# Weights handed out in 42 single pieces, and a first half batch whose operands are written in place, in a three-stage fp32 kernel

## The chip, the core and the metric

The kernel runs on one core of one Trainium2 chip. The metric is the device time of one execution in microseconds (us). Five engines work side by side, each through its own instructions in order: PE (matrix products; its weight loads are shown as PEld), DVE (vector), ACT (scalar), POOL (GpSimd) and SP, which here only issues the DMA transfers.

## The reference, cut to what matters

Inputs are float32 or, for the weights, float64 in effect (pairs of 32-bit words). Batch 4, sequence 576, 8 heads of 64, so 512 channels.

```
attn  = softmax(mask(q k^T / 8)) v                 # windowed, half the heads dilated
x     = attn as [4, 576, 512];  xp = x one row later in the sequence
xk    = mu_k x + (1 - mu_k) xp ;  xr = mu_r x + (1 - mu_r) xp
k     = relu(xk @ w_k)           # 512 -> 1024
y     = sigmoid(xr @ w_r) * ((k * k) @ w_v)        # 512 -> 512, 1024 -> 512
u     = y + (y^T U V)^T
out   = u + relu(u @ w_ch1) @ w_ch2                # 512 -> 2048 -> 512
```

## The kernel before, in words

**Stages.** The second part (r, k, v products) works on eight half batches c = 0 to 7 of 288 rows. A half batch has 20 quanta of PE work in a list (`quanta`, L525): four for r, eight for k, eight for v. Beside them run the attention of the 32 units (`attend`, L405; a unit is one pair of heads and one part of one batch) and the unpacking of the weights (`cv_bits`, L291: one ACT and four DVE instructions, L305 to L312, for a piece of 128x512). After half batch 7 comes the third part (`ch1`, `ch2`, from L688), whose weights were unpacked earlier to DRAM (`w2f`) and are read back and divided by `load_w2`.

**Two precisions.** A product of half batch 0 is one fp32 product (`mm1`, L280). It shows in the trace as two matmul instructions. From half batch 1 on each operand is divided into a high part (an ACT copy, L266) and a low part (a subtraction, L261 on POOL or L263 on DVE), and a product is three fast ones (`mm3`, L272 to L274, and L590 to L592 for v). So the 20 weight pieces of part two (4 for r, 8 for k, 8 for v) stay whole until half batch 0 has used them, and are divided for half batch 1 (`split_weight`, L331): the list `SPLIT` says after which quantum, counted from the start of half batch 1, and `SPLIT_ENG` on which engine the subtraction runs (POOL for all).

**Storage.** All operands of the products lie in one tile, `arena`, at fixed columns. In half batch 0 an unpacked piece is carried there by a transfer (L327), a mix of x by another (L520), a square of k by another (L570). The unpacked piece waits in one of three buffers `w32`, the mix in one of two `m`, the square in one of two `k2`, until its transfer has landed.

**The order around the change.** Operations are first listed in program order, each with an estimated price, and then `plan` (L129) puts them in an order per engine: it looks at most `WINDOW` operations past the oldest one not yet placed, and takes a later operation only where it can start `SLACK` ns sooner. The engines then follow that order. In the list, six steps (L790 to L795) come ahead of the quanta: each starts an attention unit, unpacks up to one more piece, and from the third step on mixes x for one pair of heads, for r and for k. Then L797 to L813 go through the quanta of half batches 0 to 6; in half batch 0 `CONV0` says how many pieces must be unpacked ahead of each quantum (7, 8, ... 20), and a new unit starts at every fifth quantum. An r quantum needs all four mixes for r and one column block of all four r weights:

```
acc = rk(XR0, [WR0 + (p // 2) * SLOT + (p % 2) * CW + o * P for p in range(NPAIR)])      # L553
dma(P * CW * 4, lambda: nc.sync.dma_start(lo, x()), kx, cols_of(col + 2 * CW, CW))      # L327
dma(P * HS * 4, lambda: nc.sync.dma_start(hi, m()), [(m,)], cols_of(c_hi, HS))          # L520
dma(P * HS * 4, lambda: nc.sync.dma_start(hi, k2()), [(k2,)], cols_of(c_hi, HS))        # L570
```

Other lines that the prediction names: L419 (scores of a unit), L464 and L475 (its transposes and its product with v), L429 (its row minimum on DVE), L454 (its normalization on POOL), L514 (a mix), L554 (an r product copied out of PSUM), L563 and L564 (relu and square of a k product), L288 and L402 (loads of packed weights and of q, k).

Of the kernel before, what the change touches and what calls it, by code (L numbers as in the profile page):

```python
# [16 lines left out]
P = 128  # L17
# [25 lines left out]
SLOT = 2048  # L43
WR0 = 0
XR0 = WR0 + 2 * SLOT
WK0 = XR0 + 8 * HS
XK0 = WK0 + 4 * SLOT
WV0 = XK0 + 8 * HS
K20 = WV0 + 4 * SLOT
ARENA = 15 * SLOT  # L50
assert K20 + 16 * HS <= ARENA

# [8 lines left out]
WHOLE = 1  # L61
# [13 lines left out]
def tile_attention_mix_channel(  # L75
# [10 lines left out]
    arena = cp.tile([P, ARENA], F32R, name="arena")  # L86
# [38 lines left out]

    def cols_of(c0, n):
        return [("arena", k) for k in range(c0 // 32, (c0 + n) // 32)]

    def plan():  # L129
# [43 lines left out]
        def ready(o):  # L173
            t = 0.0
            for d in o.deps:
                if d.done is None:
                    return None
                t = max(t, d.done + 40)
            for x in o.tiles:
                if x.ops[0] is not o and x.ops[0].done is None:  # L180
                    return None
            for x in o.first:
                if x.at and x.line[x.at - 1].ops[0].done is None and x.line[x.at - 1].ops[0] is not o:
                    return None
                ends = sorted((x_end(y) for y in x.line[max(0, x.at - 16) : x.at]), reverse=True)
# [105 lines left out]
    def cv_bits(raw, n):  # L291
        xt_ = Lazy([P, CW], F32, "w32", "w32", 3)
# [24 lines left out]
    def hi_lo(n, x, kx, c_hi, c_lo, eng):  # L317

        hi, lo = arena[:, c_hi : c_hi + n], arena[:, c_lo : c_lo + n]
        copy(n, lambda: hi, x, kx, cols_of(c_hi, n))  # L320
        sub(eng, n, lambda: lo, x, lambda: f32(hi), kx + cols_of(c_hi, n), cols_of(c_lo, n))

    def cv_weight(raw, col, whole):
        x, kx = cv_bits(raw, CW)
        if whole:
            lo = f32(arena[:, col + 2 * CW : col + 3 * CW])
            dma(P * CW * 4, lambda: nc.sync.dma_start(lo, x()), kx, cols_of(col + 2 * CW, CW))  # L327
        else:
            hi_lo(CW, x, kx, col, col + 2 * CW, "POOL")

    def split_weight(col, eng):  # L331

        lo = f32(arena[:, col + 2 * CW : col + 3 * CW])
        hi_lo(CW, lambda: lo, cols_of(col + 2 * CW, CW), col, col + 2 * CW, eng)
# [23 lines left out]
    first_slot = [Lazy([P, CW], F32R, "pr", f"w2_{j}", 4) for j in range(4)]  # L358

    def w2_part(i, part):  # L360

        if i == 0:
            return first_slot[part]()
        c = (i - 1) * SLOT + part * CW
        return arena[:, c : c + CW]

    def w2_keys(i, *parts):
        if i == 0:
            return [(first_slot[part],) for part in parts]
        return [k for part in parts for k in cols_of((i - 1) * SLOT + part * CW, CW)]  # L370

    def load_w2(i, eng):
        st = Lazy([P, 2 * CW], F32, "w64", "wst", 4)
        dma(P * CW * 8, lambda: nc.sync.dma_start(st(), w2f[i]), [("w2f", i, 0), ("w2f", i, 1)], [(st,)])
        if i == 0:
            for j in range(2):
                x = lambda j=j: st()[:, j * CW : (j + 1) * CW]
                copy(CW, lambda j=j: first_slot[j](), x, [(st,)], [(first_slot[j],)])
                sub(eng, CW, lambda j=j: first_slot[2 + j](), x, lambda j=j: f32(first_slot[j]()),
                    [(st,), (first_slot[j],)], [(first_slot[2 + j],)])  # L380
        else:
            c = (i - 1) * SLOT
            hi_lo(2 * CW, lambda: st(), [(st,)], c, c + 2 * CW, eng)
# [21 lines left out]
    def attend(u):  # L405
# [18 lines left out]
        pe(nw * 82, qk, [(raw, "qk")], [(sc,)], "qk")  # L424
# [56 lines left out]
        pe(nw * 58, pv, [(pts, 0), (raw, "v")] + ([(pts, 1)] if nw == 5 else []), [(ov,)], "pv")  # L481
# [19 lines left out]
    def mix(c, p, which):  # L501
# [6 lines left out]
        base = XK0 if which == "k" else XR0  # L508
        if (c, p) not in dd:
# [15 lines left out]
    def quanta(c):  # L525
        b, half = divmod(c, 2)
        whole = c < WHOLE
        mm = mm1 if whole else mm3
# [3 lines left out]
        vacc = {}  # L532

        def x_parts(base, p):
            return arena[:, base + p * HS : base + (p + 1) * HS], arena[:, base + (4 + p) * HS : base + (5 + p) * HS]

        def w_keys(w):
            return (cols_of(w, P) if not whole else []) + cols_of(w + 2 * CW, P)

        def x_keys(base, p, lo=4):  # L540
            return cols_of(base + p * HS, HS) + (cols_of(base + (lo + p) * HS, HS) if not whole else [])

        def rk(base, ws):
            acc = bank("M")
            trips = [
                (arena[:, w : w + P], arena[:, w + 2 * CW : w + 2 * CW + P], *x_parts(base, p)) for p, w in enumerate(ws)
            ]
            keys = [k for p, w in enumerate(ws) for k in w_keys(w) + x_keys(base, p)]
            pe(quantum_ns, lambda: mm(acc()[:, :HS], trips), keys, [(acc,)], mode)
            return acc  # L550
# [9 lines left out]
        def k_tile(o):  # L560
            acc = rk(XK0, [WK0 + p * SLOT + o * P for p in range(NPAIR)])
            rt, k2 = Lazy([P, HS], F32, "rt", "rt", 2), Lazy([P, HS], F32, "k2", "k2", 2)
            act(HS, lambda: nc.scalar.activation(rt(), acc()[:, :HS], AF.Relu), [(acc,)], [(rt,)], psum=True)  # L563
            dve(HS, lambda: nc.vector.scalar_tensor_tensor(  # L564
                out=k2(), in0=acc()[:, :HS], scalar=0.0, in1=rt(), op0=ALU.max, op1=ALU.mult),
                [(acc,), (rt,)], [(k2,)], two=True, psum=True)
            c_hi, c_lo = K20 + o * HS, K20 + (8 + o) * HS
            if whole:
                hi = f32(arena[:, c_hi : c_hi + HS])
                dma(P * HS * 4, lambda: nc.sync.dma_start(hi, k2()), [(k2,)], cols_of(c_hi, HS))  # L570
            else:
                hi_lo(HS, lambda: k2(), [(k2,)], c_hi, c_lo, "DVE" if o in K2DVE else "POOL")

        def v_part(o, part):
# [4 lines left out]
            ws = [WV0 + (j // 2) * SLOT + (j % 2) * CW + o * P for j in js]  # L579

            def run():
                a = acc()[:, :HS]
                for j, w in zip(js, ws):
                    wh, wl = arena[:, w : w + P], arena[:, w + 2 * CW : w + 2 * CW + P]
                    xh = arena[:, K20 + j * HS : K20 + (j + 1) * HS]
                    xl = arena[:, K20 + (8 + j) * HS : K20 + (9 + j) * HS]
                    if whole:
                        nc.tensor.matmul(a, lhsT=f32(wl), rhs=f32(xh), start=(j == 0), stop=(j == 7))  # L588
                        continue
                    nc.tensor.matmul(a, lhsT=wh, rhs=xh, start=(j == 0), stop=False)  # L590
                    nc.tensor.matmul(a, lhsT=wl, rhs=xh, start=False, stop=False)  # L591
                    nc.tensor.matmul(a, lhsT=wh, rhs=xl, start=False, stop=(j == 7))  # L592

            keys = [k for j, w in zip(js, ws) for k in w_keys(w) + x_keys(K20, j, 8)]
            pe(quantum_ns, run, keys, [(acc,)], mode)
# [9 lines left out]
        q = [lambda o=o: r_tile(o) for o in range(4)]  # L605
# [136 lines left out]
    cols = [WR0 + j * SLOT for j in range(2)] + [WK0 + j * SLOT for j in range(4)] + [WV0 + j * SLOT for j in range(4)]  # L742
# [5 lines left out]
    for i, j in places:  # L748
        jobs.append((w1raw[i][:, j * CW : (j + 1) * CW], CW, lambda raw, c=cols[i] + j * CW: cv_weight(raw, c, WHOLE > 0)))
# [39 lines left out]

    for t in range(FIRST + 2):  # L790
        next_unit()
        convert_to(t + 1)
        if 0 <= t - 2 < NPAIR:
            mix(0, t - 2, "r")
            mix(0, t - 2, "k")  # L795
    divided = 0
    for c in range(NCH - 1):  # L797
        cur = quanta(c)
        for n in range(NQ):
# [4 lines left out]
            cur[n]()  # L804
# [134 lines left out]
```

## Time and profile before

| | us |
|---|---|
| median of 3 runs | 825.28 (825.14 to 825.81) |
| the profiled execution's own time | 826.75 |
| its span, first to last instruction | 825.0 |
| PE busy | 788.4 (96%) |
| DVE / ACT / POOL busy | 386.6 / 326.0 / 220.6 |

The profile is one execution. The page gives busy time by engine and, in 40 slices of 20.6 us, the busy share in tenths. Other views list the instructions in order of time with the idle time ahead of each and what ended it, group them by line and shape, total the waits by engine and line, and cut the span into stretches. PE's matmuls are pipelined, so a busy PE is not PE at its peak.

### The profile page before, as it was taken

To read this page: it belongs to the slowest core of one execution; us is meant where nothing else is said; L and a number is where in the kernel's file an instruction comes from. 1 tells how busy PE (TensorE), PEld (TensorE's weight loads), DVE (VectorE), ACT (ScalarE), POOL (GpSimd) and SP (SyncE) were. 2 spreads that over 40 slices of the span, in tenths; PEclk is the share of its full clock that TensorE was granted. 3 is DMA by queue.
4 is the path that set the end of the run, shared out by engine and by line. 5 is a ranking of instruction groups with operands and counts; after the bars stand their busy time and mean duration, and the time that the engine had idled before them with its cause. 6 is when DMAs were issued, how large, how long until landed. Compare 5 with 4: busy or idle time off the path is not lost.

```text
span 825.0 us, 16083 instructions
## 1 busy us (share of the span) xinstructions
PE 788.4 (96%) x6360; PEld 752.9 (91%) x6360; DVE 386.6 (47%) x996; ACT 326.0 (40%) x848; POOL 220.6 (27%) x240
## 2 busy tenths in 40 slices
PE   4749899999999999999999999999999999999998
PEld 4527599899999999999999999999999999999998
DVE  4978778888797875345512222222222122221211
ACT  4525777575757575746411221212212112121111
POOL 1202996354545353558110010100001000110000
PEclk9999999999999999999999999999999999999999
DMA  9997434747575645043700002000020000000000
GB/s 274 278 320 251 140 122 152 236 156 222 176 227 163 223 140 182 1 131 131 237 1 29 2 1 87 1 2 29 2 73 15 1 30 1 11 19 2 29 1 29
DMA packets 39900, 85.14 MB, mean 103 GB/s; under 512 B 4496, under 2 KB 14864, under 8 KB 39824
## 3 DMA queue, kind: packets, MB, share of 16 engines
q1 hardware_dynamic: 39824, 84.10, 31.3%
q8 instruction: 50, 0.82, 0.4%
q14 instruction: 26, 0.21, 0.1%
HBM read 58.66 MB, written 17.83 MB: 93 GB/s over the span
## 4 chain that ended last, share of the span: by engine, by line
PE 92%; DMA 3%; DVE 2%; ACT 1%; issue 1%; POOL 0%; SPq 0%; ACTq 0%; POOLq 0%
PE psM L272 14%; PE psM L274 14%; PE psM L273 14%; PE psS L720 8%; PE psS L722 8%; PE psS L721 8%; PE psM L590 4%; PE psM L591 3%; PE psM L592 3%; PE psS L419 3%; PE psM L280 3%; PE psS L475 2%; PE psS L464 2%; PE psM L588 2%; DMA raw<-qk 1%; PE psM L631 1%
## 5 line engine op out<-in xcount | busy, mean ns | idle before, releaser
L700 ACT ACTIVATE ch<-psM 128x288 fp32r<-128x288 f32 x128 | 52.8, 412 | 325.4 <-PE psM L274 325.3
L701 DVE SCALAR_TENSOR_TENSOR cl<-psM,ch 128x288 fp32r<-128x288 f32 x128 | 58.4, 456 | 248.1 <-ACT ch L700 248.1
L720 PE MATMUL psS<-ch,arena 128*128 128x288 f32 x480 | 143.8, 299 | 0.0
L272 PE MATMUL psM<-uh,arena 128*128 128x288 f32 x480 | 142.3, 297 | 0.0
L722 PE MATMUL psS<-cl,arena 128*128 128x288 f32 x480 | 142.0, 296 | 0.0
L721 PE MATMUL psS<-ch,arena 128*128 128x288 f32 x480 | 141.7, 295 | 0.0
L274 PE MATMUL psM<-ul,arena 128*128 128x288 f32 x480 | 141.5, 295 | 0.0
L273 PE MATMUL psM<-uh,arena 128*128 128x288 f32 x480 | 141.4, 295 | 0.0
L261 POOL TENSOR_TENSOR ul<-u,uh 128x288 fp32r<-128x288 f32 x32 | 25.8, 807 | 322.3 <-ACT uh L266 322.3
L272 PE MATMUL psM<-arena 128*128 128x288 f32 x336 | 102.9, 306 | 0.2 <-ACT arena L266 0.2
L274 PE MATMUL psM<-arena 128*128 128x288 f32 x336 | 99.6, 296 | 0.3 <-POOL arena L261 0.3
L273 PE MATMUL psM<-arena 128*128 128x288 f32 x336 | 99.8, 297 | 0.0
L720 PEld LDWEIGHTS psS<-ch,arena 128*128 128x128 f32 x480 | 90.3, 188 | 1.1 <-issue 1.1
L273 PEld LDWEIGHTS psM<-uh,arena 128*128 128x128 f32 x480 | 90.7, 189 | 0.0
L274 PEld LDWEIGHTS psM<-ul,arena 128*128 128x128 f32 x480 | 90.5, 189 | 0.0
L721 PEld LDWEIGHTS psS<-ch,arena 128*128 128x128 f32 x480 | 90.4, 188 | 0.0
L272 PEld LDWEIGHTS psM<-uh,arena 128*128 128x128 f32 x480 | 90.2, 188 | 0.0
L722 PEld LDWEIGHTS psS<-cl,arena 128*128 128x128 f32 x480 | 90.2, 188 | 0.0
L590 PE MATMUL psM<-arena 128*128 128x288 f32 x224 | 68.9, 307 | 0.0
L261 POOL TENSOR_TENSOR arena<-m,arena 128x288 fp32r<-128x288 f32 x56 | 50.0, 903 | 64.1 <-ACT arena L266 57.3
L591 PE MATMUL psM<-arena 128*128 128x288 f32 x224 | 66.0, 295 | 0.0
L592 PE MATMUL psM<-arena 128*128 128x288 f32 x224 | 65.8, 294 | 0.0
(100 smaller groups left out, 1529.4 us busy)
## 6 DMA issues: line engine op xcount, KB each, us to landing
w<-w2raw SPq DMA_DIRECT2D x32, 512.0 KB, 5.4
w<-w1raw SPq DMA_DIRECT2D x20, 512.0 KB, 6.1
w2f<-w SPq DMA_DIRECT2D x32, 256.0 KB, 3.4
wst<-w2f SPq DMA_DIRECT2D x16, 512.0 KB, 4.0
raw<-qk SPq DMA_DIRECT2D x16, 320.0 KB, 3.6
arena<-w SPq DMA_DIRECT2D x20, 256.0 KB, 4.8
ytmp<-y SPq DMA_DIRECT2D x32, 144.0 KB, 2.8
yb<-ytmp SPq DMA_DIRECT2D x4, 1152.0 KB, 6.4
```

What stands on the lines that cost most here:

```text
L261: op("POOL", t, lambda: nc.gpsimd.tensor_tensor(out=out_(), in0=a(), in1=b(), op=ALU.subtract), r, w, 40, lock=True)
L272: nc.tensor.matmul(acc, lhsT=wh, rhs=xh, start=(i == 0), stop=False)
L273: nc.tensor.matmul(acc, lhsT=wl, rhs=xh, start=False, stop=False)
L274: nc.tensor.matmul(acc, lhsT=wh, rhs=xl, start=False, stop=(i == n - 1))
L590: nc.tensor.matmul(a, lhsT=wh, rhs=xh, start=(j == 0), stop=False)
L591: nc.tensor.matmul(a, lhsT=wl, rhs=xh, start=False, stop=False)
L592: nc.tensor.matmul(a, lhsT=wh, rhs=xl, start=False, stop=(j == 7))
L700: act(HS, lambda: nc.scalar.activation(gh(), acc()[:, :HS], AF.Relu), [(acc,)], [(gh,)], psum=True)
L701: dve(HS, lambda: nc.vector.scalar_tensor_tensor(out=gl(), in0=acc()[:, :HS], scalar=0.0, in1=f32(gh()), op0=ALU.max, op1=ALU.subtract), [ ...
L720: nc.tensor.matmul(a, lhsT=wh, rhs=gh(), start=(f == 0), stop=False)
L721: nc.tensor.matmul(a, lhsT=wl, rhs=gh(), start=False, stop=False)
L722: nc.tensor.matmul(a, lhsT=wh, rhs=gl(), start=False, stop=(f == 15))
```

## The change

The tile `arena` goes. In its place:

- 42 buffers of 128x512, handed out one at a time under the tag `w`: 20 for the whole pieces, then two (high, low) for each division, later the weights of part three. A buffer comes back when its tile's last use is over.
- Tiles `xk` (tag `A`) and `k2s` (tag `B`) for the divided mixes and squares of half batches 1 to 7, one buffer each, which part three's weights use later (`place2`). The whole mixes of half batch 0 lie in `xk0`, in one of the two buffers of the tag `x` (which hold the attention output of a batch), its whole squares in `k20`, tag `B`.
- The last DVE instruction of an unpacking writes the piece where the products read it; the mix and the square of half batch 0 too. The 20 + 8 + 8 transfers L327, L520, L570 are gone.
- In half batch 0 the r products go row by row: `r_row(p)` multiplies pair p's mix with weight piece p into four PSUM banks at once, and is listed right behind pair p's mix, in the steps ahead of the quanta. The four k mixes are listed after those steps.
- All 20 divisions subtract on DVE; `SPLIT` starts four quanta ahead of half batch 1 instead of eight. `WINDOW` goes from 60 to 100, `SLACK` from 150 to 100, and the planner's prices of scores and v products of a unit are doubled.

The diff, cut to its core:

```diff
-SLOT = 2048
...
-ARENA = 15 * SLOT
+NPIECE = 42
+XW = 16 * HS
...
-WHOLE = 1
...
-SPLIT = [-8, -7, -6, -5, -4, -3, -2, -1, 0, 1, 2, 3, 5, 5, 6, 6, 7, 7, 8, 8]
-SPLIT_ENG = ("POOL", "POOL")
+SPLIT = (-4, -4, -3, -3, -1, -1, 0, 0, 1, 1, 2, 2, 5, 5, 6, 6, 7, 7, 8, 8)
+SPLIT_ENG = ("DVE",)
...
-WINDOW = 60
-SLACK = 150.0
+WINDOW = 100
+SLACK = 100.0
...
-    arena = cp.tile([P, ARENA], F32R, name="arena")
...
+    def piece(dt, name):
+        return Lazy([P, CW], dt, "w", name, NPIECE)
...
+    def cv_weight(raw, at):
+        whole_w[at] = piece(F32, "wx")
+        cv_bits(raw, CW, whole_w[at])
+
+    def split_weight(at, eng):
+        x = whole_w[at]
+        hi, lo = hi_w[at], lo_w[at] = piece(F32R, "wh"), piece(F32R, "wl")
+        hi_lo(CW, lambda: x(), [(x,)], lambda: hi(), [(hi,)], lambda: lo(), [(lo,)], eng)
...
+        n -= 4
+        if 26 <= n < 35 or 51 <= n:
+            which, k = ("A", n - 26) if n < 35 else ("B", n - 51)
...
-        pe(nw * 82, qk, [(raw, "qk")], [(sc,)], "qk")
+        pe(nw * 168, qk, [(raw, "qk")], [(sc,)], "qk")
...
-        pe(nw * 58, pv, [(pts, 0), (raw, "v")] + ([(pts, 1)] if nw == 5 else []), [(ov,)], "pv")
+        pe(nw * 115, pv, [(pts, 0), (raw, "v")] + ([(pts, 1)] if nw == 5 else []), [(ov,)], "pv")
...
+        out_ = (lambda: xk0()[:, n * HS : (n + 1) * HS]) if c == 0 else lambda: m()
...
-            dma(P * HS * 4, lambda: nc.sync.dma_start(hi, m()), [(m,)], cols_of(c_hi, HS))
...
+    xk0 = Lazy([P, 8 * HS], F32, "x", "xk0", 2)
+    k20 = Lazy([P, 8 * HS], F32, "B", "k20", 1)
+    xk = Lazy([P, XW], F32R, "A", "xk", 1)
+    k2s = Lazy([P, XW], F32R, "B", "k2s", 1)
...
+        def r_row(p):
+
+            if p == 0:
+                racc.update((o, bank("M")) for o in range(4))
+
+            def run():
+                for o in range(4):
+                    nc.tensor.matmul(
+                        racc[o]()[:, :HS], lhsT=whole_w[p // 2, p % 2]()[:, o * P : (o + 1) * P], rhs=cols(xk0, p),
+                        start=(p == 0), stop=(p == 3),
+                    )
+
+            pe(quantum_ns, run, [(whole_w[p // 2, p % 2],), (xk0, p)], [(racc[o],) for o in range(4)], mode)
+            if p == 3:
+                for o in range(4):
+                    r_out(o, racc[o])
...
+    first = quanta(0)
     for t in range(FIRST + 2):
         next_unit()
         convert_to(t + 1)
         if 0 <= t - 2 < NPAIR:
             mix(0, t - 2, "r")
-            mix(0, t - 2, "k")
+            first[t - 2]()
+    for p in range(NPAIR):
+        mix(0, p, "k")
     divided = 0
     for c in range(NCH - 1):
-        cur = quanta(c)
+        cur = quanta(c) if c else first
         for n in range(NQ):
...
-            cur[n]()
+            if c or n >= NPAIR:
+                cur[n]()
...
```

## Rows read from the trace of the kernel before

**Rows 1.** The page: busy time by engine, then PE in 40 slices.

```profile
PE 788.4 (96%) x6360; PEld 752.9 (91%) x6360; DVE 386.6 (47%) x996; ACT 326.0 (40%) x848; POOL 220.6 (27%) x240
...
PE   4749899999999999999999999999999999999998
```

**Rows 2.** Stretches: length, busy us (instructions) per engine, granted clock, DMA share, GB/s.

```profile
0.00:44.14 44.14, 26.55 (x252) 20.78 (x252) 30.74 (x114) 22.44 (x80) 10.04 (x16) 1.00 0.93 284
44.14:64.40 20.26, 10.94 (x29) 7.66 (x30) 15.24 (x31) 5.88 (x16) 0.90 (x1) 1.00 0.89 302
64.40:106.31 41.91, 37.91 (x246) 28.68 (x244) 33.20 (x82) 28.40 (x73) 27.11 (x26) 1.00 0.56 180
106.31:146.73 40.42, 40.42 (x403) 38.30 (x401) 32.34 (x90) 28.59 (x82) 31.61 (x33) 1.00 0.45 147
```

**Rows 3.** Waits of 0 to 107 us: total, times, longest; then PE's from 107.

```profile
ACT w L305 <- DMA arena<-w: 13.0, 7, 4.7
PE psM L280 <- DMA arena<-m: 10.7, 2, 6.4
PE psM L588 <- DMA arena<-w: 3.3, 1, 3.3
...
PE psS L475 <- ACT pts L266: 1.7, 1, 1.7
```

**Rows 4.** In order of time, ACT, DVE, SP: start, length, operation [idle before].

```profile
10.46 0.43 DVE L306 TENSOR_SCALAR w<-w 128x512 f32<-128x512 f32 x1 [3.50 <-ACT w L305]
23.75 0.51 DVE L514 SCALAR_TENSOR_TENSOR m<-d,mu_t,x 128x288 f32<-128x288 f32 x1
34.22 0.76 ACT L266 ACTIVATE x<-psS 128x320 f32<-128x320 f32 x1 [0.71 <-PE psS L475]
43.42 0.69 DVE L312 SCALAR_TENSOR_TENSOR w<-w,w 128x512 int32<-128x512 int32 x1
44.14 0.47 SPq L327 DMA_DIRECT2D arena<-w  x1
49.26 0.51 DVE L514 SCALAR_TENSOR_TENSOR m<-d,mu_t,x 128x288 f32<-128x288 f32 x1
66.38 0.41 ACT L563 ACTIVATE rt<-psM 128x288 f32<-128x288 f32 x1 [2.37 <-PE psM L280]
```

**Rows 5.** PE in order of time: scores and whole products, early and late.

```profile
34.10 1.55 PE L419 MATMUL psS<-raw 64*64 64x96 f32 x16
40.43 2.29 PE L280 MATMUL psM<-arena 128*128 128x288 f32 x4
72.09 0.88 PE L419 MATMUL psS<-raw 64*64 64x96 f32 x16
...
106.31 0.51 PE L272 MATMUL psM<-arena 128*128 128x288 f32 x1
```

**Rows 6.** The chain that ended last: start, length, what.

```profile
48.77 5.97 DMA arena<-m
...
73.54 1.94 PE psM L280 x8
```

**Rows 7.** Groups by line and shape, 0 to 107 us: busy, mean ns | idle before.

```profile
L312 DVE SCALAR_TENSOR_TENSOR w<-w,w 128x512 int32<-128x512 int32 x20 | 16.3, 814 | 0.5
L554 DVE COPY sg<-psM 128x288 f32<-128x288 f32 x4 | 1.8, 453 | 2.7 <-PE psM L280 2.7
```

**Rows 8.** Line L263: the division's subtraction on DVE, 1024 columns (min/median/max ns).

```profile
L263 DVE TENSOR_TENSOR arena<-wst,arena x9: 1214/1225/1904, 382.1 to 411.1; 128x1024 fp32r<-128x1024 f32 x9
```

**Rows 9.** Stretches around the one long PE stop after 107 us (columns as rows 2).

```profile
150.00:152.00 2.00, 0.36 (x12) 0.37 (x14) 2.00 (x11) 2.00 (x7) 1.15 (x2) 1.00 0.96 336
152.00:154.00 2.00, 2.00 (x22) 1.93 (x18) 1.74 (x4) 1.79 (x10) 1.56 (x3) 0.78 0.93 269
154.00:156.00 2.00, 2.00 (x10) 2.00 (x9) 1.14 (x3) 0.86 (x3) 0.46 (x1) 0.50 0.86 307
156.00:158.00 2.00, 2.00 (x15) 2.00 (x15) 1.34 (x3) 0.00 (x0) 0.00 (x0) 0.86 0.76 262
```

More of the change, by code (lines that the diff above doesn't have):

```diff
@@ L124, in op @@
         ops.append(o)
-    def cols_of(c0, n):
-        return [("arena", k) for k in range(c0 // 32, (c0 + n) // 32)]
     def plan():
@@ L184, in ready @@
                     return None
-                ends = sorted((x_end(y) for y in x.line[max(0, x.at - 16) : x.at]), reverse=True)
+                ends = sorted((x_end(y) for y in x.line[max(0, x.at - 4 * x.bufs) : x.at]), reverse=True)
                 if len(ends) >= x.bufs:
@@ L315, in cv_bits, with hi_lo @@
         return x, kx
[L317 to L334, printed above, removed]
+    def hi_lo(n, x, kx, hi, k_hi, lo, k_lo, eng):
+        copy(n, hi, x, kx, k_hi)
+        sub(eng, n, lo, x, lambda: f32(hi()), kx + k_hi, k_lo)
+    def piece(dt, name):
+        return Lazy([P, CW], dt, "w", name, NPIECE)
+    whole_w, hi_w, lo_w = {}, {}, {}
+    def cv_weight(raw, at):
[5 more added lines that the diff above has]
+        hi_lo(CW, lambda: x(), [(x,)], lambda: hi(), [(hi,)], lambda: lo(), [(lo,)], eng)
     def cv_w2(raw, i, j):
@@ L356, in cv_v, with place2 @@
         sub("POOL", HS, lambda: v[64:96], lambda: x()[64:96], lambda: f32(v[64:96]), kx + [("vs", j)], [("vs", j)])
-    first_slot = [Lazy([P, CW], F32R, "pr", f"w2_{j}", 4) for j in range(4)]
+    parts2 = {}
+    second = {}
+    def place2(n):
+        if n < 4:
+            t = Lazy([P, CW], F32R, "pr", "w2", 4)
+            return t, 0, (t,)
+        n -= 4
+        if 26 <= n < 35 or 51 <= n:
+            which, k = ("A", n - 26) if n < 35 else ("B", n - 51)
+            if which not in second:
+                second[which] = Lazy([P, XW], F32R, which, "w2" + which, 1)
+            return second[which], k * CW, (second[which], k)
+        t = piece(F32R, "w2")
+        return t, 0, (t,)
     def w2_part(i, part):
[L362 to L365, printed above, removed]
+        t, c, _ = parts2[i][part]
+        return t()[:, c : c + CW]
     def w2_keys(i, *parts):
-        if i == 0:
-            return [(first_slot[part],) for part in parts]
-        return [k for part in parts for k in cols_of((i - 1) * SLOT + part * CW, CW)]
+        return [parts2[i][part][2] for part in parts]
     def load_w2(i, eng):
@@ L374, in load_w2 @@
         dma(P * CW * 8, lambda: nc.sync.dma_start(st(), w2f[i]), [("w2f", i, 0), ("w2f", i, 1)], [(st,)])
[L375 to L383, printed above, removed]
+        parts2[i] = [place2(4 * i + part) for part in range(4)]
+        for j in range(2):
+            hi_lo(CW, lambda j=j: st()[:, j * CW : (j + 1) * CW], [(st,)],
+                  lambda j=j: w2_part(i, j), w2_keys(i, j), lambda j=j: w2_part(i, 2 + j), w2_keys(i, 2 + j), eng)
     xt = {}
@@ L507, in mix @@
         col = 0 if which == "k" else 4
-        base = XK0 if which == "k" else XR0
+        base = 0 if which == "r" else 1
         if (c, p) not in dd:
@@ L531, in quanta @@
         sig = Lazy([P, 4, HS], F32, "sig", "sg", 1)
[L532 to L543, printed above, removed]
-            acc = bank("M")
[L545 to L550, printed above, removed]
@@ L552, in r_tile, with products @@
-        def r_tile(o):
-            acc = rk(XR0, [WR0 + (p // 2) * SLOT + (p % 2) * CW + o * P for p in range(NPAIR)])
-            dve(HS, lambda: nc.vector.tensor_copy(sig()[:, o, :], acc()[:, :HS]), [(acc,)], [(sig, o)], psum=True)
+        racc, vacc = {}, {}
+        def products(acc, trips, first=True, last=True):
+            n = len(trips)
+            keys = []
+            for i, (w, col, (xw, x, n_w, n_hi, n_lo)) in enumerate(trips):
+                if whole:
+                    keys += [(whole_w[w],), (xw, n_w)]
+                else:
+                    keys += [(hi_w[w],), (lo_w[w],), (x, n_hi), (x, n_lo)]
+            def run():
+                a = acc()[:, :HS]
+                for i, (w, col, (xw, x, n_w, n_hi, n_lo)) in enumerate(trips):
+                    start, stop = first and i == 0, last and i == n - 1
+                    c_ = slice(col, col + P)
+                    if whole:
+                        nc.tensor.matmul(a, lhsT=whole_w[w]()[:, c_], rhs=cols(xw, n_w), start=start, stop=stop)
+                        continue
+                    wh, wl, xh, xl = hi_w[w]()[:, c_], lo_w[w]()[:, c_], cols(x, n_hi), cols(x, n_lo)
+                    nc.tensor.matmul(a, lhsT=wh, rhs=xh, start=start, stop=False)
+                    nc.tensor.matmul(a, lhsT=wl, rhs=xh, start=False, stop=False)
+                    nc.tensor.matmul(a, lhsT=wh, rhs=xl, start=False, stop=stop)
+            pe(quantum_ns, run, keys, [(acc,)], mode)
@@ L556, in r_end, with r_out, r_tile @@
+        def r_out(o, acc):
+            dve(HS, lambda: nc.vector.tensor_copy(sig()[:, o, :], acc()[:, :HS]), [(acc,)], [(sig, o)], psum=True)
+        def r_tile(o):
+            acc = bank("M")
+            products(acc, [((p // 2, p % 2), o * P, (xk0, xk, p, p, 4 + p)) for p in range(NPAIR)])
+            r_out(o, acc)
         def r_end():
@@ L560, in k_tile @@
         def k_tile(o):
-            acc = rk(XK0, [WK0 + p * SLOT + o * P for p in range(NPAIR)])
-            rt, k2 = Lazy([P, HS], F32, "rt", "rt", 2), Lazy([P, HS], F32, "k2", "k2", 2)
+            acc = bank("M")
+            products(acc, [((2 + p, o // 4), o % 4 * P, (xk0, xk, 4 + p, 8 + p, 12 + p)) for p in range(NPAIR)])
+            rt = Lazy([P, HS], F32, "rt", "rt", 2)
+            k2 = None if whole else Lazy([P, HS], F32, "k2", "k2", 2)
+            sq = (lambda: cols(k20, o)) if whole else lambda: k2()
             act(HS, lambda: nc.scalar.activation(rt(), acc()[:, :HS], AF.Relu), [(acc,)], [(rt,)], psum=True)
             dve(HS, lambda: nc.vector.scalar_tensor_tensor(
[L565 to L572, printed above, removed]
+                out=sq(), in0=acc()[:, :HS], scalar=0.0, in1=rt(), op0=ALU.max, op1=ALU.mult),
+                [(acc,), (rt,)], [(k20, o) if whole else (k2,)], two=True, psum=True)
+            if not whole:
+                at(k2s, o, 8 + o, lambda: k2(), [(k2,)], "DVE" if o in K2DVE else "POOL")
         def v_part(o, part):
@@ L578, in v_part @@
             js = range(4 * part, 4 * part + 4)
[L579 to L595, printed above, removed]
+            products(acc, [((6 + j // 2, j % 2), o * P, (k20, k2s, j, j, 8 + j)) for j in js], part == 0, part == 1)
             if o == 0 and part == (1 if whole else 0):
@@ L603, in v_part @@
                     [(y,)], [("y", b, o, half)])
-        q = [lambda o=o: r_tile(o) for o in range(4)]
+        q = [lambda o=o: (r_row if whole else r_tile)(o) for o in range(4)]
         q += [lambda o=o: k_tile(o) for o in range(8)]
```

49 lines of the change are left out of this document (19 added, 30 removed).

## The prediction, made from these rows

> **What bounds the kernel now.** I read the page first, then the stretches, the waits, and last the order of time in the first 107 us. The page has PE 96% busy and, from the sixth slice on, full in nearly every slice; the other engines are far from full [rows 1]. So the end is set by PE, and time is only to be had where PE stands. The waits say where: before 107 us PE stands, besides its waits for early attention, for landings of mixes (10.7 us) and of a weight piece (3.3 us); after 107 us for 1.7 us, once [rows 3]. The stretches say it by stage [rows 2]: half batch 1 runs from 106.31 to 146.73 with PE full for all 40.42 us; the stretch ahead of it, k and v products of half batch 0, is 41.91 us with 37.91 busy; and in the 20.26 us ahead of that PE is busy for 10.94, with few instructions. So what counts is **X, the start of half batch 1, now 106.31** [rows 5]: behind it lies a fixed amount of PE work, and a microsecond that X comes sooner is one at the end, unless new stops eat it.
>
> What sets X? The last two mixes are computed at 48.23 and 49.26 [rows 4], though attention wrote their x at 34.22 (the fourth and last copy of 320 rows, L266) [rows 4]: each mix waits for one of two `m` buffers, which a transfer holds. The transfer issued at 48.77 takes 5.97 us, and only then, at about 54.75, do r products run without a gap [rows 6]. The first relu of a k product starts at 66.38 [rows 4], and a product of eight instructions takes 1.94 us [rows 6], so k products start at about **T = 64.4**. DVE is busy for 30.74 of the first 44.14 us, and about 9.5 us of its 13.4 us of idle time lie ahead of 10.46 [rows 2, 4]; it is the engine that PE's start will rest on once transfers no longer do.
>
> **Part 1: r by rows, mixes in place (T).** r's 16 products are 32 instructions, 7.8 us at the late rate of 1.94/8 and 18.3 us at the early one of 2.29/4 [rows 5, 6]. They move into steps where PE has gaps. Of the moved mixes every issue counts: eight transfers leave SP's queue. The four r copies on DVE (0.45 each [rows 7]) move ahead of the first k product too, which needs their PSUM banks. T then rests on the later of two things.
> DVE: the eighth piece, the last that the first k product needs, is unpacked at 44.14 [rows 4]. Three mixes that now come later must come ahead of it (3 x 0.51 [rows 4] = 1.5) and four copies (1.8): 47.4. At most the 3.9 us of DVE idle time between 10.46 and 44.14 can be won back: 43.5.
> PE: row 0 can start when the first mix is done, at 24.3 [rows 4]. PE is busy for 26.55 us of the first 44.14 [rows 2], all attention but for 2.29 of r [rows 5]; about half of that, 12 us, comes after 24.3 (an estimate: three units of six). With r at the late rate 24.3 + 12 + 7.8 = 44.1, at the early rate 54.6.
> I take **T = 48**, between the two PE ends and by the DVE row; ends 43.5 and 55.
> The rows print a granted clock of 1.00 there, yet 16 scores take 1.55 us at 34.10 and 0.88 at 72.09 [rows 5], so I go by durations. [...]
>
> **Part 2: pieces in place (from T to X).** 20 transfers go, and with them ACT's 13.0 us of waits for an unpacking buffer and PE's last 3.3 us [rows 3]; SP loses 36 issues of some 0.47 us, several of which stood waiting for DVE with weight loads behind them. Loads of q and k keep waiting in SP's queue for a free buffer as before.
> PE's side: 37.91 us of work after T [rows 2], X = 86.
> DVE's side: 15.24 + 33.20 = 48.4 us of work from 44.14 to 106.31 [rows 2], less what moved ahead of T (3.3), plus eight divisions. A division's subtraction on DVE has a row with 1024 columns, 1.225 us [rows 8]; half is 0.61, so +4.9. Sum 50.0. POOL sheds its divisions, and DVE instructions stretch beside POOL's: L312 takes 0.69 alone [rows 4] and 0.81 in the mean [rows 7]; I take 3 us of relief, ends 0 and 5, and 1 us of work that X does not need. That is 46 us: **X = 48 + 46 = 94**, ends 86 (PE's side) and 99. DVE, not PE, is the later one here, so PE will have some gaps. The gain at X is 12.3 us.
> Waits added: a division needs two of 42 pieces. Ahead of half batch 1 at most 20 + 2 x 8 = 36 are out, and r's whole pieces return at once; nothing. `k2s` waits for the last v product that reads `k20`; the k product ahead of it stands behind that on PE anyway. The next batch's x waits for `xk0` or the old x, both read to the end a quantum stage earlier. [...]
>
> **Part 3: half batch 1.** DVE is busy 32.34 of 40.42 us [rows 2]. Twelve divisions add 7.3: 39.7, less up to 4 of relief. That is nearly full. [...] I take 1 us for part of one; ends 0 and two stops, 7. The old stop at 150 us may stay or go (0 to 3.4 gained); I let it stay, since nothing in the change is aimed at its cause, an ACT copy of attention.
> [...]
>
> **Part 4: the rest.** From half batch 2 on no line changes but for storage. A third-part weight's last two pieces can wait for the first four k products of half batch 7 instead of its r products, some 6 us later; it is used over ten quanta on. The planner's new window and prices reorder all engines; after 107 us PE stands for 1.7 us in all [rows 3], so there is nothing to gain and up to a stop or two to lose: 0, ends +3.4 and -3.4.
>
> **Sum.** The profiled execution has a span of 825.0 and a time of 826.75, 1.5 above the median of 825.28. 825.0 - 12.3 + 1.0 = 813.7 of span; against the median **814.0**.
>
> **The rivals.**
> *Both engines keep up.* The quick rate comes early, T is 44 and X between 86 and 89, DVE gets its relief, and the stop at 150 goes. 825.3 - 17.5 to 23: 802 to 808. For it: idle time on DVE early, and gapless r rows. Against: DVE's sum of 46 us. Chance 0.17.
> *Rows get in the way.* At the early rate a row takes 4.6 us of PE ahead of a unit's transposes; units fall behind, DVE's row minima wait in its queue with the unpacking behind them, SP's loads of the next units wait with weight loads behind. T is 55 and X 98 to 102, with a stop: 817 to 824. For it: PE's early rate and chains of attention in the trace. Chance 0.18.
> *Slower: DVE full means PE stop and go.* [...] For it: DVE's 39.7 of 40.4 us. Against: PE has a list to choose from, and with DVE busy for 32.34 of 40.42 us [rows 2] it makes no stop at all. Chance 0.10.
> *The transfers were covered.* If T hangs on attention, which is not touched, the transfers lay beside it and only the 3.3 us wait goes: 822 to 825. Against: x of the last pair was there 14 us ahead of its mixes. Chance 0.07.
>
> **How the numbers follow.** The forecast, X from 91 to 97 with at most a stop more, gives 810 to 818 and has 0.48. A measurement here can tell 0.2%, 1.7 us. Faster: 0.48 + 0.17 + 0.17 + 0.03 = 0.85; same 0.05, from the last rival and the edge of the second; slower 0.10. The range, 803.5 to 822, leaves out the best end of the first rival and the worst of the others, about 2 in 10.
>
> **What would show it.** Right: no transfer into operands; r products between 25 and 48; first k product near 48; half batch 1 at 91 to 97; DVE over 90% busy from 48 to 135. Wrong in part 1: four-instruction bursts of r at 2.3 us apiece to the end and T past 54. Wrong in part 2: the last piece unpacked later than 85. Wrong in part 3: stretches of clock 0.50 after X. Wrong in the whole: X past 104, or new PE waits after half batch 2.

## The result, and the profile after

The changed kernel takes **806.17 us** (median of 4 runs, 804.72 to 807.25) against 825.54 for the kernel before: a ratio of 0.9763, 95% interval 0.9743 to 0.9783, or 19.4 us less. The profiled execution is the 804.72 one, with a span of 802.9.

The page after, for [rows 1]:

```profile
PE 776.3 (97%) x6360; PEld 743.9 (93%) x6360; DVE 385.3 (48%) x1025; ACT 325.6 (41%) x863; POOL 201.3 (25%) x226
...
PE   5878999999999999999999999999999999999998
```

PE is full from the fifth slice on, and its busy time fell by 12 us without one product less. Half of that lies ahead of half batch 1, though more attention is done there now: early instructions take longer (four took 2.29 us [rows 5], eight later ones 1.94 [rows 6]), and fewer go at that rate. Stretches after, for [rows 2], cut at the moment the eighth piece is unpacked, at the start of half batch 1, and 40 us behind it:

```profile
0.00:45.75 45.75, 30.76 (x322) 23.36 (x322) 32.49 (x132) 25.75 (x91) 12.57 (x18) 1.00 0.82 247
45.75:90.00 44.25, 38.67 (x247) 29.37 (x248) 42.48 (x111) 29.50 (x77) 15.81 (x15) 0.96 0.61 189
90.00:130.00 40.00, 40.00 (x381) 38.25 (x381) 37.64 (x98) 32.27 (x85) 20.15 (x23) 1.00 0.41 126
```

The same moments in order of time (in the changed file L293 is the last unpacking instruction, L563 a row of r, L547 a whole k or v product, L591 the relu of a k product, L550 the first divided product):

```profile
21.82 2.21 PE L563 MATMUL psM<-xk,wx 128*128 128x288 f32 x8
...
44.44 1.31 DVE L293 SCALAR_TENSOR_TENSOR wx<-w,wx 128x512 int32<-128x512 int32 x1
45.81 6.57 PE L547 MATMUL psM<-xk,wx 128*128 128x288 f32 x26 [1.89 <-DVE wx L293]
48.52 0.41 ACT L591 ACTIVATE rt<-psM 128x288 f32<-128x288 f32 x1
...
80.66 9.72 PE L547 MATMUL psM<-k,wx 128*128 128x288 f32 x32
81.10 0.68 DVE L293 SCALAR_TENSOR_TENSOR wx<-w,wx 128x512 int32<-128x512 int32 x1
90.00 0.51 PE L550 MATMUL psM<-xk,wh 128*128 128x288 f32 x1
```

By the first relu, k products begin 17.9 us sooner (66.38 to 48.52), so T is 46.5. PE's own row puts it at 45.8, when the eighth piece is there: the relu stood behind a copy on ACT that had waited for a load of weights. X, the start of half batch 1, is 90.0 instead of 106.3. DVE is busy for 42.48 of the 44.25 us between the eighth piece and X. The last piece is unpacked at 81.78 (81.10 + 0.68). PE's waits, for [rows 3], all of the run:

```profile
PE psS L463 <- ACT pts L253: 10.1, 10, 2.3
PE psS L407 <- DMA raw<-qk: 8.8, 3, 4.5
PE psM L547 <- DVE wx L293: 3.7, 3, 1.9
```

No wait for a transfer into an operand is left. Besides early loads of q and k, what PE waits for now is DVE's unpacking and attention, whose chain also goes through DVE.

From X to the end the changed kernel needs 712.9 us (802.9 - 90.0) against 718.7; the stretches, before and after:

```profile
106.31:825.00 718.69, 712.98 (x5838) 695.78 (x5836) 307.42 (x772) 269.25 (x681) 182.56 (x199) 1.00 0.25 82
90.00:802.90 712.90, 706.87 (x5793) 691.14 (x5791) 310.31 (x785) 270.36 (x696) 172.97 (x194) 1.00 0.25 81
```

PE has 45 instructions less to do there: one attention unit more is through ahead of X (eleven have their scores there instead of ten), some 2.6 us. The stop that [rows 9] show came back, 1.69 us at 131, but the printed clock stays at 1.00 behind it, so the 1.7 us of slow products went. The other 1.5 us lie in PE's busy time, and their cause stays open; what PE waits for behind X is alike, 2.2 us before and 2.3 after.

### The profile page after: what moved, and what is told of

It reads as the page before. It is cut to its first block, busy times and chain, and to the rows that moved or that the text cites. A ratio compares the mean times of both kernels' runs of the same rounds, so it can differ in the third digit from the quotient of the medians.

```text
span 802.9 us, 15981 instructions
## 1 busy us (share of the span) xinstructions
PE 776.3 (97%) x6360; PEld 743.9 (93%) x6360; DVE 385.3 (48%) x1025; ACT 325.6 (41%) x863; POOL 201.3 (25%) x226
## 4 chain that ended last, share of the span: by engine, by line
PE 91%; DMA 3%; DVE 3%; ACT 2%; issue 1%; SPq 0%; POOL 0%; ACTq 0%; POOLq 0%
PE psM L550 10%; PE psM L552 9%; PE psM L551 9%; PE psS L728 9%; PE psS L729 8%; PE psM L260 8%; PE psM L259 8%; PE psS L730 8%; PE psM L261 8%; PE psS L407 3%; PE psS L463 2%; PE psS L452 2%; DMA w<-w1raw 1%; PE psM L547 1%; DMA raw<-qk 1%; PE psM L639 1%
## 5 line engine op out<-in xcount | busy, mean ns | idle before, releaser
L728 PE MATMUL psS<-ch,w 128*128 128x288 f32 x384 | 114.7, 299 | 0.0
L259 PE MATMUL psM<-uh,w 128*128 128x288 f32 x384 | 113.4, 295 | 0.0
L261 PE MATMUL psM<-ul,w 128*128 128x288 f32 x384 | 113.3, 295 | 0.0
L730 PE MATMUL psS<-cl,w 128*128 128x288 f32 x384 | 113.3, 295 | 0.0
L248 POOL TENSOR_TENSOR ul<-u,uh 128x288 fp32r<-128x288 f32 x32 | 27.1, 848 | 321.6 <-ACT uh L253 321.6
L729 PE MATMUL psS<-ch,w 128*128 128x288 f32 x352 | 103.8, 295 | 0.0
L260 PE MATMUL psM<-uh,w 128*128 128x288 f32 x352 | 103.7, 295 | 0.0
L550 PE MATMUL psM<-xk,wh 128*128 128x288 f32 x336 | 101.8, 303 | 0.0
L552 PE MATMUL psM<-xk,wh 128*128 128x288 f32 x336 | 99.4, 296 | 0.0
L551 PE MATMUL psM<-xk,wl 128*128 128x288 f32 x336 | 98.2, 292 | 0.0
L728 PEld LDWEIGHTS psS<-ch,w 128*128 128x128 f32 x384 | 72.4, 188 | 0.0
L730 PEld LDWEIGHTS psS<-cl,w 128*128 128x128 f32 x384 | 72.3, 188 | 0.0
L259 PEld LDWEIGHTS psM<-uh,w 128*128 128x128 f32 x384 | 72.3, 188 | 0.0
L550 PE MATMUL psM<-k2s,wh 128*128 128x288 f32 x224 | 68.9, 308 | 0.0
L552 PE MATMUL psM<-k2s,wh 128*128 128x288 f32 x224 | 66.2, 296 | 0.0
L729 PEld LDWEIGHTS psS<-ch,w 128*128 128x128 f32 x352 | 66.2, 188 | 0.0
L260 PEld LDWEIGHTS psM<-uh,w 128*128 128x128 f32 x352 | 66.1, 188 | 0.0
```

Source lines behind the costliest of these rows:

```text
L248: op("POOL", t, lambda: nc.gpsimd.tensor_tensor(out=out_(), in0=a(), in1=b(), op=ALU.subtract), r, w, 40, lock=True)
L259: nc.tensor.matmul(acc, lhsT=wh, rhs=xh, start=(i == 0), stop=False)
L260: nc.tensor.matmul(acc, lhsT=wl, rhs=xh, start=False, stop=False)
L261: nc.tensor.matmul(acc, lhsT=wh, rhs=xl, start=False, stop=(i == n - 1))
L550: nc.tensor.matmul(a, lhsT=wh, rhs=xh, start=start, stop=False)
L552: nc.tensor.matmul(a, lhsT=wh, rhs=xl, start=False, stop=stop)
```

## The experiments

Twelve runs, one of them the changed kernel again. Each edited kernel goes through the planner again, so an edit also moves instructions that it does not name; a difference below about 2 us is not read as the edit's own. Nor is one below about 3 us in X, which is read from a single profile: the changed kernel has 90.0 in the first and 87.3 in the second. Differences are taken from ratios to the kernel before on the same chip (that one ran between 825.5 and 827.3), times 825.5. The changed kernel itself has 0.9763 and, run again, 0.9754.

**The planner alone.** The kernel before with the new numbers:

```diff
-WINDOW = 60
-SLACK = 150.0
+WINDOW = 100
+SLACK = 100.0
...
-        pe(nw * 82, qk, [(raw, "qk")], [(sc,)], "qk")
+        pe(nw * 168, qk, [(raw, "qk")], [(sc,)], "qk")
...
-        pe(nw * 58, pv, [(pts, 0), (raw, "v")] + ([(pts, 1)] if nw == 5 else []), [(ov,)], "pv")
+        pe(nw * 115, pv, [(pts, 0), (raw, "v")] + ([(pts, 1)] if nw == 5 else []), [(ov,)], "pv")
```

> The kernel before with only the planner's new window, slack and prices of scores and v products. Theory (the gain is from operands written in place and from r row by row): the first k product stays near 64 and the time at 825, within 2 us. Rival (the planner's new order brings the gain): half of the 19 us or more, 815 or less.

824.28 us, ratio 0.9982 (0.9969 to 0.9995): 1.5 us less. The first relu of a k product came at 60.1 instead of 66.4, which the theory did not expect. X came at 109.4, 3 us later, and from there to the end the kernel needs 712.9 us with 5793 PE instructions, just what the changed kernel needs: the new numbers bring a unit forward, and X comes later by about as much. And the reverse, the changed kernel with the old numbers:

> The changed kernel with the old window, slack and prices. Theory (storage and rows carry the gain): 806 to 810. Rival (the new order carries it): 815 or more, with new stops of PE.

809.76 us, ratio 0.9796 (0.9776 to 0.9817): some 3 us more than the changed kernel, though the two intervals touch. X is 90.2, the same; the loss comes behind it, where the unit's 45 PE instructions stand again:

```profile
90.20:805.70 715.50, 710.42 (x5838) 693.43 (x5836) 315.31 (x797) 273.60 (x705) 175.74 (x196) 1.00 0.25 82
```

The new order is a small part of the gain, not its carrier.

**Rows of r undone.**

```diff
-        q = [lambda o=o: (r_row if whole else r_tile)(o) for o in range(4)]
+        q = [lambda o=o: r_tile(o) for o in range(4)]
...
-            first[t - 2]()
...
-            if c or n >= NPAIR:
-                cur[n]()
+            cur[n]()
```

> The changed kernel with r of half batch 0 by tiles again, listed behind the six steps; mixes and pieces still in place. Theory (the rows take 7.8 us of PE out of the way of the k products): half batch 1 starts 5 to 8 us later than the 90.0 of the changed kernel, 811 to 815. Rival (DVE's unpacking sets the start of half batch 1 whatever PE does): same start, 805 to 808.

805.61 us, ratio 0.9745 (0.9717 to 0.9773), X 89.5: the rival. The lines of PE in order of time, cut at 36 us, say why:

```profile
35.62 7.91 PE L547 MATMUL psM<-xk,wx 128*128 128x288 f32 x23
...
44.08 9.97 PE L547 MATMUL psM<-xk,wx 128*128 128x288 f32 x40
```

With r by tiles, r's 32 instructions run from 35 to about 46 us and straight on into the k products (8 and 32 of the last 40), and PE waits for no piece in this run. With rows, r is done at 39.9, and PE waits for the eighth piece until 45.81. The rows take work out of a stretch in which PE has nothing else.

**Divisions back on POOL, at the old places.**

```diff
-SPLIT = (-4, -4, -3, -3, -1, -1, 0, 0, 1, 1, 2, 2, 5, 5, 6, 6, 7, 7, 8, 8)
-SPLIT_ENG = ("DVE",)
+SPLIT = [-8, -7, -6, -5, -4, -3, -2, -1, 0, 1, 2, 3, 5, 5, 6, 6, 7, 7, 8, 8]
+SPLIT_ENG = ("POOL", "POOL")
```

> The changed kernel with the divisions on POOL and their old places. Theory (as in the prediction: 12 us less on a full DVE, but stretched beside POOL, so nearly even): half batch 1 within 3 us of 90.0, 804 to 810. Rival 1 (DVE's load is what holds it): 802 or less. [...]

814.40 us, ratio 0.9866 (0.9836 to 0.9896): 9 us lost, X 100.1: more than the theory (810 at most) and the rival (802 at most) allow. PE stands for the last piece, which DVE has ready at 91.1 instead of 81.8:

```profile
91.20 9.28 PE L547 MATMUL psM<-k,wx 128*128 128x288 f32 x26 [7.00 <-DVE wx L293]
```

DVE by line from 41.7 to 90 us, first the changed kernel, then this one (busy us, mean ns):

```profile
L290 DVE SCALAR_TENSOR_TENSOR wx<-w,wx 128x512 int32<-128x512 int32 x14 | 10.5, 750 | 0.0
L293 DVE SCALAR_TENSOR_TENSOR wx<-w,wx 128x512 int32<-128x512 int32 x14 | 10.3, 736 | 0.0
L250 DVE TENSOR_TENSOR wl<-wx,wh 128x512 fp32r<-128x512 f32 x8 | 7.2, 909 | 0.1
L287 DVE TENSOR_SCALAR wx<-wx 128x512 f32<-128x512 f32 x12 | 5.4, 453 | 0.1
...
L288 DVE TENSOR_SCALAR wx<-wx 128x512 int32<-128x512 int32 x12 | 4.9, 409 | 0.0
```

```profile
L293 DVE SCALAR_TENSOR_TENSOR wx<-w,wx 128x512 int32<-128x512 int32 x14 | 13.0, 927 | 0.1
L290 DVE SCALAR_TENSOR_TENSOR wx<-w,wx 128x512 int32<-128x512 int32 x14 | 11.8, 845 | 0.1
L288 DVE TENSOR_SCALAR wx<-wx 128x512 int32<-128x512 int32 x14 | 8.2, 593 | 0.1
L287 DVE TENSOR_SCALAR wx<-wx 128x512 f32<-128x512 f32 x12 | 7.1, 595 | 0.0
```

Freed of eight divisions (7.2 us), DVE spends 8.3 us more on the same unpacking instructions (0.191 x 14 + 0.095 x 14 + 0.184 x 14 + 0.142 x 12). Seen singly, POOL and then DVE in order of time:

```profile
78.32 4.52 POOL L248 TENSOR_TENSOR wl<-wx,wh 128x512 fp32r<-128x512 f32 x3
```

```profile
78.67 1.38 DVE L288 TENSOR_SCALAR wx<-wx 128x512 int32<-128x512 int32 x1
80.08 1.64 DVE L290 SCALAR_TENSOR_TENSOR wx<-w,wx 128x512 int32<-128x512 int32 x1
81.76 1.64 DVE L293 SCALAR_TENSOR_TENSOR wx<-w,wx 128x512 int32<-128x512 int32 x1
```

Beside three POOL subtractions of 1.5 us each, DVE's instructions, 0.41 and 0.69 us long otherwise, take about as long as POOL's do. A division on POOL was not taken off DVE here.

**The engine without the places.** The changed kernel with `SPLIT_ENG = ("POOL",)` and nothing else.

> The changed kernel with the divisions on POOL at the new places. Theory (a division beside DVE on POOL costs DVE about as much as one on DVE, and takes longer itself): 809 to 815, the loss now in half batch 1. Rival (the early places made the loss of the POOL run, not the engine): 804 to 808.

815.14 us, ratio 0.9865 (0.9835 to 0.9896): 9 us lost again. X is 93.8 here and the rest goes behind it, 717.1 us instead of 712.9, with 5.7 us of waits of PE instead of 2.3. It is the engine, not the places.

**POOL's subtractions without anyone who waits for them.** This kernel adds work that the output does not use:

```diff
+    scr = Lazy([P, CW], F32, "scr", "scr", 1)
+    op("POOL", 300, lambda: nc.gpsimd.memset(scr(), 1.0), [], [(scr,)], 40)
...
+            while idle < 12 and (c - 1) * NQ + n + 1 >= idle - 8:
+                sub("POOL", CW, lambda: scr(), lambda: scr(), lambda: scr(), [(scr,)], [(scr,)])
+                idle += 1
```

> The changed kernel with twelve subtractions of 512 columns on POOL from the eighth quantum ahead of half batch 1 on, one per quantum, on a tile of their own that nobody waits for. Theory (POOL's subtractions hold up DVE's instructions beside them by themselves): DVE's unpacking instructions stretch, half batch 1 starts 4 to 7 us later, 809 to 813. Rival (it was the wait for a division's slower result): 805 to 807, DVE's means as in the changed kernel.

822.61 us, ratio 0.9940 (0.9917 to 0.9963): 15 us lost, more than the theory's 4 to 7; X is 101.0. That POOL's subtractions stretch DVE's instructions by themselves is settled, for nobody waits for these results. Two of them, and two DVE instructions beside them (a mix, 0.51 us otherwise, and one of 0.41):

```profile
84.47 2.25 POOL L248 TENSOR_TENSOR scr<-scr 128x512 f32<-128x512 f32 x2
```

```profile
84.54 1.28 DVE L504 SCALAR_TENSOR_TENSOR m<-d,mu_t,x 128x288 f32<-128x288 f32 x1 [0.69 <-POOL xk L248]
85.74 1.26 DVE L288 TENSOR_SCALAR wx<-wx 128x512 int32<-128x512 int32 x1
```

The size is not fully explained. By the means up to 100 us, DVE's unpacking takes 5.9 us longer (0.220 x 12 + 0.171 x 12 + 0.059 x 13 + 0.028 x 14). PE's waits for attention grew from 10.1 to 19.3 us, with stops of up to 6.1 us. The subtractions also stand in POOL's queue ahead of work that others do wait for, and the planner, which keeps these POOL and DVE instructions from overlapping in its plan, put the work in another order; how much of the 15 us is due to these two was not separated.

**Divisions on DVE alone.** The kernel before with the new `SPLIT` and `("DVE", "DVE")`.

> The kernel before with the divisions on DVE at the new places, nothing else. Theory (DVE's sum decides, and this part gives about 8 us by itself): 815 to 820. Rival (it only pays once transfers are gone, since these still hold up unpacking): 822 to 827.

817.92 us, ratio 0.9884 (0.9867 to 0.9900): 9.6 us, half of the whole gain, from this one part, with all transfers still there. X is 100.5. PE has no gap from 53.2 us to X; its wait of 3.3 us for the last piece [rows 3] is gone, though the piece is still carried.

**Transfers put back, one kind at a time.**

```diff
-        cv_bits(raw, CW, whole_w[at])
+        x, kx = cv_bits(raw, CW)
+        dma(P * CW * 4, lambda: nc.sync.dma_start(whole_w[at](), x()), kx, [(whole_w[at],)])
```

> The changed kernel with the 20 transfers of weight pieces put back (unpacked into one of three buffers, then carried). Theory (they hold up unpacking: 13 us of ACT waits, SP's queue): half batch 1 starts 6 to 10 us later, 812 to 817. Rival (they lay beside other work): 804 to 808.

811.17 us, ratio 0.9815 (0.9782 to 0.9848): 5 us, a little under the range of the theory; X 95.5. The waits that came back, PE's and ACT's up to 107 us:

```profile
PE psM L548 <- DMA wx<-w: 6.7, 3, 4.1
```

```profile
ACT w L286 <- DMA wx<-w: 11.0, 10, 2.3
```

And the mixes of half batch 0, through `m` and a transfer into `xk0`:

```diff
-        m = None if c == 0 else Lazy([P, HS], F32, "m", "m", 2)
+        m = Lazy([P, HS], F32, "m", "m", 2)
...
+        if c == 0:
+            dma(P * HS * 4, lambda: nc.sync.dma_start(xk0()[:, n * HS : (n + 1) * HS], m()), [(m,)], [(xk0, n)])
```

> The changed kernel with the eight transfers of half batch 0's mixes put back (two buffers). Theory (the last mixes wait for buffers held by transfers): first k product about 50 to 53 instead of 41.7, half batch 1 5 to 8 us later, 811 to 815. Rival (unpacking sets it): 804 to 808.

807.75 us, ratio 0.9775 (0.9750 to 0.9800), 1.7 us more, which the intervals don't separate from none. The first relu of a k product comes at 54.1 instead of 48.5, as the theory said, yet X is 89.9, the same within what is read:

```profile
52.23 17.13 PE L548 MATMUL psM<-xk,wx 128*128 128x288 f32 x58 [3.67 <-DMA xk<-m]
```

From 52.2 us on PE has no gap up to X, so here its own work sets X. It starts later and waits less: behind its earlier start the changed kernel's PE stands for 1.6 us for a piece and for 4.0 us for attention. The eight transfers of squares were not tried by themselves.

**PE's rate.** Eleven idle products in PE's waits ahead of 12 us, beside a second run of the changed kernel:

```diff
...
+    def warm(n):
+        for _ in range(n):
+            pe(MM1, lambda: nc.tensor.matmul(wb()[:, :HS], lhsT=wt()[:, :P], rhs=wt()[:, P : P + HS], start=True, stop=True),
+               [(wt,)], [(wb,)], "f32")
...
+    warm(3)
     a_load(0)
...
+        if t == 0:
+            warm(8)
```

> The changed kernel once more, for runs on the same chip as the next three: 804.7 to 807.3 as before. Open: whether PE's quick rate begins at about 20 us again (it began at 61 in the kernel before); if that moment moves from run to run, the spread of 2.5 us may come from it.

> The changed kernel with eleven idle products on PE in its waits ahead of 10 us (nothing else changed). Theory (PE's slow rate lengthens the first attention units, which the rest of the prologue follows): quick rate from about 5 us, first k product 2 to 3 us sooner, 802 to 804. Rival (loads and DVE set the prologue): 805 to 807, but with the quick rate early and less spread.

806.13 and 805.65 us, ratios 0.9754 (0.9714 to 0.9795) and 0.9757 (0.9717 to 0.9798): no difference, nor in X (87.3 and 87.1). PE with the idle products, in order of time:

```profile
1.35 4.21 PE L781 MATMUL psM<-warm 128*128 128x288 f32 x8 [1.35 <-DVE warm L777]
5.49 1.38 PE L407 MATMUL psS<-raw 64*64 64x96 f32 x20
...
17.73 1.04 PE L407 MATMUL psS<-raw 64*64 64x96 f32 x20 [1.08 <-DMA raw<-qk]
```

The quick rate is there from about 6 us (twenty scores take 1.04 instead of 1.86), and the run is no faster, nor is its spread smaller (804.2 to 809.9). So the rate in the prologue sets nothing, and it does not explain the spread. Part of what does shows in the two profiles of the changed kernel. In the second:

```profile
78.91 0.80 PE L463 MATMUL psS<-pts,raw 96*64 96x64 f32 x20 [2.37 <-ACT pts L253]
79.64 8.03 PE L547 MATMUL psM<-k,wx 128*128 128x288 f32 x32
```

In the first the same stop is 2.30 us long, and the same 32 instructions behind it take 9.72 us at a granted clock that falls to 0.50; in the second they take 8.03. That is 1.7 of the 2.7 us by which X differs. Why they were slow once and not again stays open.

**A step further.** Since POOL's subtractions cost DVE, half batch 1's mixes were divided on DVE too:

```diff
-            at(xk, 8 * base + p, 8 * base + 4 + p, lambda: m(), [(m,)], "POOL")
+            at(xk, 8 * base + p, 8 * base + 4 + p, lambda: m(), [(m,)], "DVE" if c == 1 else "POOL")
```

> The changed kernel with the eight low parts of half batch 1's mixes on DVE too (0.4 us each) instead of POOL (1.1 us each). Theory (what POOL sheds DVE gains back): half batch 1 starts 0 to 2 us sooner, 803 to 806. Rival (each one adds to the fullest engine): 3 us later, 808 to 809.

809.56 us, ratio 0.9792 (0.9753 to 0.9831), X 92.2: by the median 3 us slower, as the rival said, though the interval reaches into that of the changed kernel. The rival's reason does not show on DVE. Up to X the eight subtractions cost it 3.6 us (0.45 each), and its other instructions, divisions, mixes and L290 above all, win about as much back by their means. What PE stands for ahead of X is attention:

```profile
82.22 1.30 PE L452 MATMUL psS<-cst_t,pr 128*96 128x128 f32 x5 [3.83 <-POOL pr L442]
```

Whether that wait comes of the move or of the new order was not separated. No variant is clearly faster than the changed kernel.

## Why the prediction was right, and where its terms were off

The direction and the range (803.5 to 822) held, but the forecast of 814.0 gave 11.3 us where 19.4 were measured; the time fell into the range of the first rival, which had 0.17. Half of that rival came true: the quick rate came early (from about 21 us, ahead of the first row of r at 21.82) and X lay near its 86 to 89, but T was not 44, and PE still waited for pieces. So the range held by the end that was kept for this rival, not by the forecast's own sum. In the profiled pair the miss is 4.0 us at X (94 to 90.0) and 6.8 behind it (1.0 lost was taken, 5.8 were won), less 2.7 that are the choice of execution.

- *What bounds it.* Right. X moved by 16.3 us and the end by 22.1, with PE full behind X but for a few waits. And DVE is the later engine ahead of X: what leaves DVE alone (rows, the mixes' transfers, PE's rate) did not move X, what stretches or holds up its unpacking (POOL's work, the pieces' transfers) did. But it is the later one by little: with the rows undone or the mixes carried, PE waits for no piece any more, and X is the same.
- *Part 1.* T was put at 48 and came at about 46, by the DVE row as said. That the rows of r matter for it was wrong: undone, they cost nothing. PE's ends, 44 to 55, hung on a rate that turned out not to count. And the old T was not all transfers: with the planner's numbers alone, the first relu came 6.3 us sooner, and DVE is at work right up to the two late mixes (no idle time ahead of 48.23 and 49.26 [rows 4]), so no buffer is seen to hold them.
- *Part 2, mis-sized.* "I take 3 us of relief, ends 0 and 5." By the same sum (48.4 - 3.3 + 4.9 - 1, against 42.5 us measured) DVE did with 6.5 us less, beyond the upper end, although a division took 0.91 us in this stretch and not 0.61. Not all of this is relief from POOL. The durations of DVE's instructions add up to 54.3 us before (44.14 to 106.31) and 52.0 after (45.75 to 90.0), while its busy times are 48.5 and 42.5: neighbours overlap, by 5.8 us before and by 9.5 after. With the divisions back on POOL the overlap is 9.0 (47.7 to 100.1), so POOL does not make it. So 3.7 of the 6.5 us are overlap, which the sum has at nothing; the rest, 2.8, is near the 3 taken, and is what is left of a larger relief once the dearer divisions (8 x 0.3) are paid. How large the stretch was, the mean of L312 over all of the first 107 us [rows 7] hid, since 13 of its 20 instances end ahead of 64.4 us, where POOL is busy for 10.9 us in all [rows 2], and take 0.69 in the mean. The others, beside 27.1 us of POOL's work:

```profile
L312 DVE SCALAR_TENSOR_TENSOR w<-w,w 128x512 int32<-128x512 int32 x7 | 7.3, 1045 | 0.2
```

  So X was 90 and not 94, about half of it by T. That moving the divisions is the largest single part, 9 to 10 us, was not foreseen at all: the text treated it as a cost.
- *Part 3.* A loss of 1 us was taken, the author's estimate for part of a stop. No run shows it: half batch 1 has DVE busy for 37.6 of 40 us, as worked out (39.7 less relief), and PE does not stop in those 40 us. The 1.7 us of slow products behind the old stop went, which the text had let stay.
- *Part 4, the term that failed.* No new wait of PE above 0.7 us came behind 140, as said. But "there is nothing to gain" from the planner's new numbers looked at PE's stops alone. They bring a whole unit's products ahead of X, 2.6 of the 5.8 us won from X to the end, and the kernel before with these numbers alone has the same 712.9 us behind X.
- *The slower rival* did not come. One stop of 2.3 us ahead of X did, with the clock behind it:

```profile
78.00:80.00 2.00, 0.07 (x2) 0.07 (x4) 2.00 (x13) 2.00 (x8) 1.38 (x2) 1.00 0.49 147
80.00:82.00 2.00, 2.00 (x24) 1.60 (x25) 2.00 (x3) 1.78 (x6) 1.27 (x2) 0.85 0.12 22
82.00:84.00 2.00, 2.00 (x6) 1.35 (x5) 1.97 (x4) 0.62 (x2) 1.64 (x2) 0.50 0.91 245
84.00:86.00 2.00, 2.00 (x8) 1.55 (x7) 2.00 (x5) 0.66 (x2) 0.14 (x1) 0.80 0.68 264
```

PE idles from 77.6 to 79.9, and the granted clock is 0.85, 0.50 and 0.80 in the three stretches behind. The 3.4 us taken for a stop came from the one in [rows 9], 1.7 idle and some 1.7 behind it; it was about right for this one (2.3 idle and 1.7 in slow products), and four such stops would be needed to eat up the 12.3 us expected at X. As a price for every stop it was too high: the one at 131 and the second profile's of 2.37 us cost their idle time alone.
- *The two executions.* 2.7 us of the 22.1 in span are the choice of execution: the profiled one is 1.5 us below its median, the one before 1.2 above.

Undoing the parts one by one gives 9 (divisions), 5 (pieces' transfers), 3 (planner), at most 2 (mixes, not told from none) and nothing (rows), some 17 to 19 us together. That leaves no large part of the 19.4 without a name, though single undos need not add up.

## What to carry to other kernels

Work put on POOL was not free for DVE here (L288 took 0.41 us alone and 1.38 beside POOL's subtractions): look at single DVE instructions beside POOL's before calling it offloaded, and not at a mean over a long stretch. Where one engine supplies another, ask which of the two is late in the stretch ahead of the full one; edits on the early one (rows, an earlier start, a quicker rate) bought nothing here. An order that brings work forward can pay (some 3 us here) although the full engine stops no less. A buffer that is only free when a transfer has landed can hold up the producer (ACT, for 11.0 us with the pieces' transfers back), not just the reader (PE, for 6.7).

## What the runs showed of the hardware that was not expected

- POOL's subtractions with two inputs stretched DVE's instructions to about their own length, including some that read one tensor: L288 took 0.41 us alone and 1.38 beside POOL subtractions of 1.5. DVE's row minima, which read PSUM, were not stretched: 0.24 to 0.25 us each from 83.31 us on in the run with POOL's divisions, beside a subtraction of 1.68 at 82.84. By what means POOL holds DVE up was not shown. It was the size that was not expected: the kernel with twelve subtractions that nobody waits for, 14 us of POOL time, is 15 us slower, of which 5.9 are seen as longer unpacking on DVE.
- PE's early attention products stayed at the slow rate for very different times in kernels that begin alike: they were quick from about 21 us in the changed kernel (16 scores in 0.88 us at 23.96), from about 61 in the one before (whole products: six instructions in the 2 us from 58, ten in those from 62). The printed clock reads 1.00 in both.
- A stop of about 1.7 us at 150 was followed by a granted clock down to 0.50 in the kernel before, and one of 1.69 at 131 by a clock of 1.00 in the changed one. One of 2.30 us at 78 was followed by 0.50 in the first profile of the changed kernel, and 32 instructions took 9.72 us; behind one of 2.37 in the second they took 8.03.
